# Hash attention with a feed-forward block: the first batch's value sums on GpSimd, with the order of the work made anew

## The chip, the cores and the metric

The kernel runs on one core of a Trainium2 chip. The core has five engines that run side by side, each through its own queue of instructions: TensorE (PE in the profile, with its weight loads as PEld), VectorE (DVE), ScalarE (ACT), GpSimd (POOL) and SyncE (SP), which here only issues DMAs. The metric is the device time of one execution in microseconds (us); lower is better.

## The reference

Four batches, eight heads, 768 positions, head size 64. Six random projections hash every query and key to a bucket; a query attends only to keys of its own bucket. Layer norm and a feed-forward block with a residual follow.

```python
q_bits = (np.einsum('bhsd,dk->bhsk', q, proj) > 0)      # k_bits alike
mask = q_bucket[:, :, :, None] == k_bucket[:, :, None, :]
scores = np.where(mask, scale * np.matmul(q, k.transpose(0, 1, 3, 2)), -1e9)
attn = np.exp(scores - scores.max(-1, keepdims=True))
attn = attn / (attn.sum(-1, keepdims=True) + 1e-09)
x = np.matmul(attn, v)                        # heads side by side: (4, 768, 512)
xn = (x - mu) / np.sqrt(var + 1e-06) * g_ln
out = x + np.maximum(xn @ w_ch1, 0.0) @ w_ch2   # 512 -> 2048 -> 512
```

Where no key shares a query's bucket, every score is -1e9 and the result is the plain mean of the values. The kernel reproduces this by adding 2^-100 times the sum of all values (and of as many ones) to every row of the attention product: it vanishes beside a real attention sum and decides where that is nothing. These sums of values over the keys, one vector for each head, are what the change is about.

## The kernel before

The work is cut into 12 query blocks u of 256 queries (three for each batch) and into two groups g of four heads. A step s of 72 takes one block, one group and one third of the keys. The whole kernel is one string, `ORDER` (lines 16 to 136), of words such as `A.t.5.2`: the operation, the engine whose queue it enters (t TensorE, v VectorE, a ScalarE, p GpSimd, s SyncE), and its arguments. The program walks through the words and emits each operation; so the string fixes the order in every engine's queue, and each engine takes its own words strictly in that order. Dependencies between engines are semaphores. `SLOTS` (139 to 163) says which of the few buffers of a kind (`pp` and `f` are PSUM places, `X`, `T`, `tp`, `vnat` and so on SBUF buffers) each new tile takes, in the order in which tiles are made.

The words that matter here, with the lines of their code:

- First batch, queries and keys: `lx` loads (370, buffers X), `tn` turns 32x32 blocks on DVE (375), `ca` casts to bfloat16 (382, the queue is the word's engine; the cast itself is line 311, 313 or 315), `ha` or `hc` multiply with the projections in float32 (392, 402), `bh`, `bc`, `sl`, `bi` make the sign bits from that (396 to 430).
- Later batches: `gx` (504) is a tiny GpSimd write that waits until an X buffer is free, `LX` (507) the load into it, `tu` the turning (510), `CA` the cast (518), `hm` the projection (521), `bt`, `mw`, `mr` the bits and their way through DRAM (534 to 551).
- Scores `S` (558), exponentials `E` in two halves (575), attention products `A` (587), and on DVE `na` (606, adds the value sums, empties the accumulator), `nb` (612, reciprocal and multiplication at line 617), `nc` and `ag` (statistics), `rs` (634, GpSimd: the inverse deviation), `ce` (626, centring), `fl` (638, a transposing DMA) or, for block 0, `ft` and `fc` through TensorE.
- Feed-forward: `F` (652) first product, `R` (662) ReLU on ACT or DVE, and for block 0 `D` and `Z` (669, 674), for the others seven smaller products `P`, `Y` (715 to 728) with sums of weights `sw` (688) and of activations `ss` (699). `lw1` and `lw2` load the quarters of the two weights through GpSimd's DMA queue (445, 456), `wg` scales a quarter of the first weight by the layer norm's gain (448). `O` writes results.
- Values: `lv` loads them (463), `cv` casts two heads to bfloat16 into `vaug` (469).

Value sums are made in two ways. `sq` (491), used for batch 0 only, multiplies a matrix of ones with each of the six pieces of the cast values on TensorE. `su` (477), used for batches 1 to 3, first adds the six pieces in float32 on GpSimd, and `sp` (486) then needs one ones product, which sums over the partitions. `sc` (496) copies either result from PSUM.

```python
    def su(eng, b, hs):
        ...
        nc.gpsimd.tensor_tensor(t3, s[:, 0:3], s[:, 3:6], op=AOP.add)
        nc.gpsimd.tensor_tensor(t3[:, 0], t3[:, 0], t3[:, 1], op=AOP.add)
        nc.gpsimd.tensor_tensor(
            vsum(b)[:, D * hs : D * (hs + 4)].rearrange("p (h d) -> p h d", d=D), t3[:, 0], t3[:, 2], op=AOP.add,
        )
    def sp(eng, b, hs):
        nc.tensor.matmul(
            ps(f"vp{b}{hs}", [P, 512], "f")[:, :256], ones, vsum(b)[:, D * hs : D * (hs + 4)], start=True, stop=True,
        )
    def sq(eng, b, hs):
        ...
        for kj in range(KJ):
            nc.tensor.matmul(p, ones, vaug(b)[:, hs : hs + 4, kj, 0:D], start=(kj == 0), stop=(kj == KJ - 1))
```

`wm` words are products of ones with ones that fill TensorE's queue during the first 11 us.

## Time and profile before

| | us |
|---|---|
| median of three runs | 294.56 (293.67 to 295.48) |
| the profiled execution | 294.45 |
| its span, first to last instruction | 292.7 |
| TensorE idle in the span | 8.2 |
| first feed-forward product group ready to go on (L657) | 36.79 |
| last product ends (L723) | 288.4 |

The granted TensorE clock was 0.999 over the span. A profile line names a source line, an engine, an operation, and output and input tiles with shapes; `x6` is a count, and an arrow in square brackets names what ended the engine's idle time before. "The chain of waits" is the profile's reconstruction, from the last instruction backwards, of what each step waited for. The tables of stretches give busy microseconds of each engine in a window; a busy TensorE need not be TensorE at its peak, since the ends of its pipelined products are modelled.

### The profile page before, as it was taken

The page shows a single profiled execution, that of the slowest core. Times are in us where ns is not written, and L with a number is a line of the kernel's source. Part 1 is how long each engine was busy: PE and PEld are TensorE (multiplying, and loading weights), DVE is VectorE, ACT ScalarE, POOL GpSimd, SP SyncE. Part 2 cuts the span into 40 slices and gives each one's busy share as a digit, 9 for nine tenths or more (in the row PEclk, how much of TensorE's full clock was granted, in tenths as well). Part 3 has the DMA queues.
Part 4 walks back from the last instruction along what each step waited for, and adds up shares of the span by engine and source line. Part 5 has one row for each costly group of instructions (what it writes and reads, how often), then busy time and mean ns, then how long its engine had stood idle before and what let it go on. Part 6 is the DMA issues. An engine that isn't in the chain of part 4 may idle for free.

```text
span 292.7 us, 10520 instructions
## 1 busy us (share of the span) xinstructions
PE 284.5 (97%) x4650; PEld 227.0 (78%) x4650; DVE 211.8 (72%) x475; ACT 199.8 (68%) x229; POOL 59.5 (20%) x94
## 2 busy tenths in 40 slices
PE   8999999999899999999999999999999999999994
PEld 4677778568688787888888878888888888898883
DVE  4889999876978978777577787467486566872543
ACT  2699898887956886775964996597784483715230
POOL 6353502133521100410510100602301000101000
PEclk9999999999999999999999999999999999999999
DMA  6996999589964580381930570130320201304032
GB/s 216 295 394 114 198 280 185 121 122 235 261 172 114 149 198 15 87 189 37 210 87 17 128 107 20 39 74 2 75 40 0 56 20 41 88 0 110 4 87 73
DMA packets 31055, 34.10 MB, mean 116 GB/s; under 512 B 15521, under 2 KB 27809, under 8 KB 31010
## 3 DMA queue, kind: packets, MB, share of 16 engines
q1 hardware_dynamic: 25938, 28.72, 39.1%
q0 software_dynamic: 4224, 4.19, 9.0%
q8 instruction: 36, 0.59, 0.8%
q10 hardware_dynamic: 848, 0.53, 0.7%
q14 instruction: 9, 0.07, 0.1%
HBM read 27.86 MB, written 6.88 MB: 119 GB/s over the span
## 4 chain that ended last, share of the span: by engine, by line
PE 92%; DVE 4%; DMA 2%; issue 0%
PE f L657 28%; PE sc L570 18%; PE X L723 13%; PE acc L595 12%; PE Yb L723 7%; PE Ya L723 3%; PE f L672 3%; PE hp L526 2%; DMA xnT<-xc 2%; PE hf L394 2%; PE warm L363 1%; DVE w_sb L454 1%; PE warm L366 1%; DVE x L617 1%; PE vp L494 0%; DVE st L621 0%
## 5 line engine op out<-in xcount | busy, mean ns | idle before, releaser
L576 ACT ACTIVATE E<-sc,bias_sb 128x1024 bf16<-128x1024 f32 x144 | 153.3, 1111 | 38.2 <-PE sc L570 35.5
L657 PE MATMUL f<-xnT,w_sb 128*128 128x256 bf16 x768 | 93.9, 273 | 1.9 <-DMA xnT<-xc 1.2
L657 PEld LDWEIGHTS <-w_sb 128*128 128x128 bf16 x768 | 71.8, 98 | 15.2 <-issue 4.5
L665 ACT ACTIVATE hb<-f 128x512 bf16<-128x512 f32 x64 | 37.9, 597 | 36.6 <-PE f L657 36.3
L570 PE MATMUL sc<-qb,kb 32*128 32x256 bf16 x1152 | 52.2, 267 | 0.0
L595 PE MATMUL acc<-vaug,E 128*128 128x65 bf16 x1152 | 43.4, 194 | 0.0
L595 PEld LDWEIGHTS <-E 128*128 128x128 bf16 x1152 | 40.7, 98 | 3.4 <-issue 2.5
L570 PE MATMUL sc<-G 6*128 6x256 bf16 (+1 forms) x576 | 41.5, 273 | 0.6 <-DVE G L307 0.5
L723 PEld LDWEIGHTS <-hb 128*128 128x128 bf16 x352 | 32.9, 98 | 6.0 <-issue 1.9
L635 POOL TENSOR_SCALAR rs<-mv 128x2 f32<-128x2 f32 x12 | 2.8, 232 | 157.7 <-DVE mv L624 157.7
L667 DVE TENSOR_SCALAR hb<-f 128x512 bf16<-128x512 f32 x32 | 21.8, 681 | 16.3 <-PE f L657 16.0
L728 DVE TENSOR_TENSOR x<-X,x 128x256 f32<-128x256 f32 x44 | 18.4, 421 | 18.1 <-PE X L723 17.9
L570 PEld LDWEIGHTS <-kb 32*128 32x128 bf16 x1152 | 30.2, 93 | 1.6
L723 PEld LDWEIGHTS <-S 128*128 128x128 bf16 x264 | 25.0, 98 | 4.7 <-issue 0.8
L570 PEld LDWEIGHTS <-G 6*128 6x128 bf16 (+1 forms) x576 | 15.2, 91 | 16.2 <-issue 13.5
L304 DVE STREAM_TRANSPOSE T<-X 128x384 f32<-128x384 f32 (+2 forms) x52 | 26.3, 539 | 0.0
L723 PE MATMUL Yb<-w_sb,S 128*128 128x256 bf16 x176 | 22.9, 273 | 0.0
L608 DVE SCALAR_TENSOR_TENSOR y<-vsB,acc 128x520 f32<-128x520 f32 x24 | 16.6, 690 | 7.4 <-PE acc L595 7.1
L723 PE MATMUL X<-wt,hb 128*128 128x256 bf16 x168 | 21.8, 273 | 0.0
L617 DVE TENSOR_TENSOR x<-y,rc 128x512 f32<-128x512 f32 x24 | 17.5, 731 | 0.8
L621 DVE BATCH_NORM_STATS2 st<-x 128x6 f32<-128x256 f32 x48 | 17.7, 412 | 0.2
L480 POOL TENSOR_TENSOR t<-vn 128x768 f32<-128x768 f32 x6 | 10.9, 1818 | 20.0 <-DMA vn<-in_v_dram 20.0
(92 smaller groups left out, 269.2 us busy)
## 6 DMA issues: line engine op xcount, KB each, us to landing
out_dram<-x SPq DMA_DIRECT2D x45, 128.0 KB
X<-in_k_dram SPq DMA_DIRECT2D x7, 768.0 KB
X<-in_q_dram SPq DMA_DIRECT2D x6, 768.0 KB
vn<-in_v_dram SPq DMA_DIRECT2D x24, 192.0 KB
w_sb<-in_moe_w_ch_dram POOLq DMA_DIRECT2D x8, 512.0 KB, 8.9
vn<-in_v_dram SPq DMA_DIRECT2D x2, 768.0 KB
X<-in_q_dram SPq DMA_DIRECT2D x2, 512.0 KB
Bd<-B SPq DMA_DIRECT2D x6, 96.0 KB
```

The costliest lines, as they stand in the source:

```text
L304: nc.vector.transpose(d[:, j], s[:, j, kj0 : kj0 + n])
L570: nc.tensor.matmul(sc(s, i // 2)[:, i % 2, 256 * kk : 256 * kk + 256], lh, rh, start=(rep == 0), stop=(rep == 2), skip_group_check=True,)
L576: nc.scalar.activation(E(s)[:, heads(h)], sc(s, h), AF.Exp, scale=EXP_SCALE, bias=bias_sb)
L595: nc.tensor.matmul(acc[:, qt, (D + 1) * i : (D + 1) * (i + 1)], E(s)[:, i, 256 * kk + P * qt : 256 * kk + P * qt + P], vaug(u // 3)[:, 4 * ...
L608: nc.vector.scalar_tensor_tensor(yt(u, g), vs, EPS_ROW, made[f"acc{u}{g}"][:, :, :A], op0=AOP.mult, op1=AOP.add,)
L617: nc.vector.tensor_tensor(xo, a[:, :, :, 0:D], rc.to_broadcast([P, 2, 4, D]), op=AOP.mult)
L621: nc.vector.bn_stats(stats(u)[:, qt, g], xt(u)[:, qt, 256 * g : 256 * g + 256])
L657: nc.tensor.matmul(f1[:, n].rearrange("p (t x) -> p t x", t=2), w1_sb[:, dt, P * nt : P * nt + P], xnT(u)[:, :, dt], start=(dt == 0), stop ...
L665: nc.scalar.activation(hb(u)[:, 2 * p : 2 * p + 2], f1, AF.Relu)
L667: eng.tensor_scalar_max(hb(u)[:, 2 * p : 2 * p + 2], f1, 0.0)
L723: nc.tensor.matmul(f2, lh[:, n], rh[:, n], start=(first and n == 0), stop=(n == 7), skip_group_check=True)
L728: nc.vector.tensor_tensor(x, made[f"{prod(u, k)}{u}"], x, op=AOP.add)
```

## The change

In batch 0 the two `sq` words are replaced by two `su` words on GpSimd and two `sp` words on TensorE. `ORDER` and `SLOTS` are written anew throughout: almost every line of the order differs, words move within their queues, and some change the engine (up to about 40 us: casts `ca.0.1.2`, `ca.1.1.2` from GpSimd and `ca.0.0.2` and the copy `bi.1.0.2` from ACT to DVE; `ca.1.1.0` from DVE to GpSimd; `ca.1.1.1`, `cv.0.0.2` and the ReLU `R.0.7` from DVE to ACT; `cv.0.4.0` from GpSimd to ACT). No function changes. The diff's first part and the buffers named here, cut:

```diff
@@ -16,147 +16,147 @@
...
-tn.v.1.1.1 ha.t.1.1.1 tn.v.1.0.0 E.a.1.1 gx.p.1.0.0 S.t.2.2 LX.s.1.0.0 E.a.2.0 ca.v.1.1.0 ha.t.1.0.0
-bh.v.1.1.1 ca.v.1.0.0 ha.t.1.1.0 ca.v.1.1.1 bh.v.1.0.0 cv.p.0.0.0 tn.v.1.1.2 cv.v.0.0.2 S.t.4.2 E.a.2.1
-E.a.4.0 E.a.4.1 gx.p.1.0.1 tn.v.0.0.2 ca.a.0.0.2 bh.v.1.1.0 A.t.2.2 sq.t.0.0 LX.s.1.0.1 sc.v.0.0
-A.t.1.2 A.t.0.2 ca.p.1.1.2 tn.v.0.0.1 ca.a.0.0.1 gx.p.1.1.1 S.t.3.2 ha.t.1.1.2 E.a.3.0 cv.p.0.4.0
-na.v.0.0 hc.t.0.0.1 nb.v.0.0 E.a.3.1 bh.v.1.1.2 bc.v.0.0.1 S.t.5.2 E.a.5.1 sl.t.0.0.1 tn.v.1.0.2
-bi.v.0.0.1 cv.p.0.4.2 sq.t.0.4 tn.v.1.0.1 E.a.5.0 sc.v.0.4 hc.t.1.0.2 S.t.8.2 E.a.8.0 gx.p.1.1.0
-tu.v.1.0.0.2 bc.v.1.0.2 hc.t.1.0.1 lw1.p.1 tu.v.1.0.0.3 A.t.4.2 tu.v.1.0.0.0 A.t.3.2 E.a.8.1 bc.v.1.0.1
-lw1.p.2 sl.t.1.0.1 bi.a.1.0.1 A.t.5.2 tu.v.1.0.0.1 tu.v.1.0.1.2 lw1.p.0 sl.t.1.0.2 bi.a.1.0.2 ca.a.1.0.1
...
-ce.v.0.0 ce.v.0.1 pmem.p rs.p.0 gt.t E.a.7.1 A.t.7.2 A.t.6.2 A.t.8.2 bt.v.1.0
-gc.v E.a.9.0 E.a.9.1 ft.t.0.1 fc.a.0.1 wg.v.1 ft.t.0.0 fc.a.0.0 lw2.p.1 S.t.10.2
-E.a.10.0 E.a.10.1 na.v.1.0 F.t.0.3 wg.v.3 wg.v.2 R.a.0.3 S.t.11.2 F.t.0.7 E.a.11.0
...
-lw2.p.0 S.t.12.2 R.a.0.6 na.v.1.1 lv.s.1.0.3 nb.v.1.1 E.a.12.1 CA.p.1.0.1 tu.v.1.1.0.2 mr.s.1.0.3
-E.a.13.0 lw2.p.3 mr.s.1.0.0 A.t.14.2 A.t.12.2 R.v.0.0 F.t.0.5 F.t.0.2 rs.p.1 tu.v.1.1.0.0
-tu.v.1.1.1.0 tu.v.1.1.0.1 ce.v.1.1 A.t.13.2 na.v.2.0 ca.a.1.0.2 nb.v.2.0 lw2.p.2 S.t.16.2 R.a.0.2
...
-nc.v.2.0 lv.s.1.0.1 sw.v.1.1 mr.s.1.1.2 A.t.17.2 A.t.15.2 E.a.18.1 A.t.16.2 na.v.2.1 D.t.0.1.2
-sw.v.3.0 mr.s.1.1.1 S.t.20.2 E.a.20.0 cv.a.1.0.2 nb.v.2.1 nc.v.2.1 E.a.20.1 D.t.0.0.2 D.t.0.0.3
-Z.v.0.0 S.t.19.2 E.a.19.0 D.t.0.1.3 Z.v.0.1 mr.s.1.1.0 E.a.19.1 fl.s.1.0 mr.s.1.1.3 lv.s.1.4.3
-su.p.1.0 F.t.1.4 R.v.1.4 lv.s.1.4.2 S.t.21.2 E.a.21.0 E.a.21.1 F.t.1.2 cv.p.1.0.0 LX.s.2.0.1
-R.a.1.2 lv.s.1.4.0 F.t.1.0 ag.v.2.1 R.a.1.0 A.t.20.2 sw.v.2.0 A.t.19.2 ag.v.2.0 rs.p.2
-ce.v.2.1 sw.v.4.1 ce.v.2.0 S.t.22.2 E.a.22.1 lv.s.2.0.1 LX.s.2.0.0 fl.s.2.1 sp.t.1.0 F.t.1.3
-R.a.1.3 sc.v.1.0 A.t.18.2 cv.a.1.4.2 na.v.3.0 tu.v.2.0.1.2 F.t.1.5 O.s.0.1 R.v.1.5 F.t.1.6
-R.v.1.6 sw.v.1.0 fl.s.2.0 E.a.22.0 nb.v.3.0 S.t.23.2 E.a.23.1 su.p.1.4 F.t.1.7 cv.v.1.4.0
-R.a.1.7 LX.s.3.1.0 E.a.23.0 tu.v.2.0.0.1 F.t.1.1 S.t.24.2 F.t.2.1 R.v.1.1 ss.v.1.1 ss.v.1.2
...
+sel.p tn.v.0.0.0 p32.p tn.v.0.1.0 on.p.1 lw1.p.3 ca.a.0.0.0 pmem.p ca.p.0.1.0 ha.t.0.0.0
...
+tn.v.1.1.1 E.a.1.0 ha.t.0.1.2 ha.t.1.1.1 bh.v.0.1.2 tn.v.1.1.0 ca.p.1.1.0 S.t.2.2 ca.a.1.1.1 tn.v.1.0.0
+ha.t.1.0.0 E.a.2.0 cv.a.0.0.2 bh.v.1.1.1 ca.v.1.0.0 bh.v.1.0.0 tn.v.1.1.2 ha.t.1.1.0 bh.v.1.1.0 tn.v.0.0.2
+tn.v.0.0.1 S.t.4.2 ha.t.1.1.2 cv.p.0.0.0 E.a.2.1 A.t.2.2 E.a.4.0 su.p.0.0 hc.t.0.0.1 bc.v.0.0.1
+A.t.1.2 bh.v.1.1.2 sl.t.0.0.1 E.a.4.1 ca.v.1.1.2 ca.a.0.0.1 cv.a.0.4.0 S.t.3.2 gx.p.1.0.1 sp.t.0.0
+bi.v.0.0.1 LX.s.1.0.1 A.t.0.2 E.a.3.0 su.p.0.4 gt.t sc.v.0.0 E.a.3.1 na.v.0.0 tn.v.1.0.2
+gc.v S.t.5.2 E.a.5.0 S.t.8.2 E.a.5.1 E.a.8.0 E.a.8.1 tn.v.1.0.1 nb.v.0.0 hc.t.1.0.1
+tu.v.1.0.0.1 sp.t.0.4 tu.v.1.0.0.3 tu.v.1.0.0.2 cv.p.0.4.2 A.t.4.2 bc.v.1.0.1 sl.t.1.0.1 bi.a.1.0.1 sc.v.0.4
+tu.v.1.0.0.0 tu.v.1.0.1.1 ca.a.1.0.1 tu.v.1.0.1.3 A.t.5.2 A.t.3.2 na.v.0.1 nb.v.0.1 lw1.p.2 tu.v.1.0.1.2
+S.t.6.2 E.a.6.0 hc.t.1.0.2 S.t.7.2 E.a.6.1 E.a.7.1 E.a.7.0 lw1.p.1 tu.v.1.0.1.0 hm.t.1.0
+S.t.9.2 E.a.9.0 nc.v.0.1 nc.v.0.0 bc.v.1.0.2 ag.v.0.0 sl.t.1.0.2 ag.v.0.1 A.t.7.2 ce.v.0.1
+bt.v.1.0 ce.v.0.0 bi.v.1.0.2 lw1.p.0 lw2.p.0 E.a.9.1 wg.v.2 A.t.6.2 A.t.8.2 na.v.1.0
+ft.t.0.1 fc.a.0.1 mw.s.1.0 mr.s.1.0.1 ft.t.0.0 fc.a.0.0 S.t.10.2 E.a.10.0 mr.s.1.0.0 wg.v.3
+hc.t.0.0.2 bc.v.0.0.2 F.t.0.4 S.t.11.2 R.v.0.4 ca.v.0.0.2 E.a.10.1 sl.t.0.0.2 bi.v.0.0.2 wg.v.0
...
+S.t.16.2 mr.s.1.0.3 E.a.16.1 lv.s.1.0.3 ag.v.1.1 ag.v.1.0 E.a.16.0 rs.p.1 R.a.0.6 A.t.14.2
+lw2.p.1 A.t.12.2 lv.s.1.0.1 F.t.0.5 lv.s.1.4.2 tu.v.1.1.0.0 R.a.0.5 tu.v.1.1.1.3 tu.v.1.1.1.0 lw2.p.2
+A.t.13.2 tu.v.1.1.0.2 tu.v.1.1.0.3 S.t.15.2 tu.v.1.1.0.1 E.a.15.1 lw2.p.3 tu.v.1.1.1.2 na.v.2.0 E.a.15.0
...
+na.v.2.1 nb.v.2.1 sw.v.3.1 sw.v.1.0 S.t.20.2 E.a.20.0 D.t.0.1.2 D.t.0.0.2 mr.s.1.1.1 cv.v.1.0.0
+D.t.0.0.3 E.a.20.1 S.t.19.2 E.a.19.1 E.a.19.0 Z.v.0.0 LX.s.2.0.1 cv.p.1.0.2 su.p.1.0 D.t.0.1.3
+nc.v.2.1 Z.v.0.1 LX.s.2.1.0 lv.s.1.4.3 lv.s.1.4.1 F.t.1.4 R.a.1.4 S.t.21.2 E.a.21.1 nc.v.2.0
+ag.v.2.1 ag.v.2.0 sw.v.2.0 F.t.1.2 R.v.1.2 F.t.1.0 E.a.21.0 R.v.1.0 A.t.18.2 lv.s.1.4.0
+A.t.20.2 rs.p.2 ce.v.2.0 ce.v.2.1 fl.s.2.1 sw.v.1.1 F.t.1.3 R.a.1.3 fl.s.2.0 sw.v.2.1
+sw.v.4.1 O.s.0.3 A.t.19.2 sp.t.1.0 sc.a.1.0 S.t.22.2 F.t.1.6 E.a.22.0 E.a.22.1 na.v.3.0
+F.t.1.5 S.t.23.2 E.a.23.0 R.v.1.6 R.v.1.5 F.t.1.7 F.t.1.1 R.a.1.7 E.a.23.1 R.v.1.1
+S.t.24.2 E.a.24.1 E.a.24.0 tu.v.2.0.1.2 LX.s.2.0.0 LX.s.2.1.1 F.t.2.1 O.s.0.0 cv.p.1.4.0 cv.v.1.4.2
...
-    T="011001100110",
-    X="0123021302312012",
-    rs="012102102102",
-    vnat="01010101",
-    vsum="000",
...
+    T="011001011010",
+    X="0123021302310312",
+    rs="012012012012",
+    vnat="01010110",
+    vsum="0000",
...
```

GpSimd's queue up to the second batch, before and after:

```
before: on.0 sel p32 on.1 lw1.3 ca.0.1.0 ca.0.1.1 ca.0.1.2 gx.1.0.0 cv.0.0.0 gx.1.0.1 ca.1.1.2 gx.1.1.1 cv.0.4.0 cv.0.4.2 gx.1.1.0
        lw1.1 lw1.2 lw1.0 pmem rs.0 lw2.1 lw2.0 CA.1.0.1 lw2.3 rs.1 lw2.2 CA.1.1.1 su.1.0 cv.1.0.0 rs.2
after:  on.0 sel p32 on.1 lw1.3 pmem ca.0.1.0 ca.0.1.1 gx.1.0.0 ca.1.1.0 cv.0.0.0 su.0.0 gx.1.0.1 su.0.4 cv.0.4.2
        lw1.2 lw1.1 lw1.0 lw2.0 CA.1.0.1 gx.1.1.1 gx.1.1.0 rs.1 lw2.1 lw2.2 lw2.3 rs.0 cv.1.0.2 su.1.0 rs.2
```

TensorE's queue around the replaced products, before and after:

```
before: S.4 A.2 sq.0.0 A.1 A.0 S.3 ha.1.1.2 hc.0.0.1 S.5 sl.0.0.1 sq.0.4 hc.1.0.2 S.8 hc.1.0.1 A.4 A.3 sl.1.0.1 A.5 sl.1.0.2 S.6 hc.0.0.2 sl.0.0.2
        S.7 hm.1.0 S.9 gt A.7 A.6 A.8 ft ft S.10 F.0.3 S.11
after:  S.4 ha.1.1.2 A.2 hc.0.0.1 A.1 sl.0.0.1 S.3 sp.0.0 A.0 gt S.5 S.8 hc.1.0.1 sp.0.4 A.4 sl.1.0.1 A.5 A.3 S.6 hc.1.0.2
        S.7 hm.1.0 S.9 sl.1.0.2 A.7 A.6 A.8 ft ft S.10 hc.0.0.2 F.0.4 S.11
```

More of the change, by code (lines that the diff above doesn't have):

```diff
@@ new lines @@
+S.t.57.2 ss.v.6.3 sc.a.3.0 E.a.57.1 fl.s.7.0 F.t.7.5 R.a.7.5 Y.v.6.1 na.v.9.0 P.t.6.6
+Y.v.6.6 S.t.59.2 E.a.57.0 E.a.59.1 E.a.59.0 P.t.6.5 Y.v.6.5 P.t.6.7 Y.v.6.7 S.t.60.2
+E.a.60.0 P.t.6.3 nc.v.8.1 P.t.6.4 ag.v.8.1 A.t.59.2 Y.v.6.3 ag.v.8.0 sp.t.3.4 Y.v.6.4
+O.s.6.2 rs.p.8 E.a.60.1 sc.v.3.4 S.t.61.2 E.a.61.1 E.a.61.0 F.t.7.6 R.v.7.6 A.t.58.2
+A.t.57.2 nb.v.9.0 F.t.7.4 S.t.64.2 F.t.7.0 R.a.7.4 E.a.64.0 na.v.9.1 nb.v.9.1 R.v.7.0
+A.t.60.2 nc.v.9.1 E.a.64.1 F.t.7.7 R.a.7.7 F.t.7.2 R.v.7.2 S.t.62.2 E.a.62.1 nc.v.9.0
@@ new lines @@
+F.t.7.1 ce.v.8.0 fl.s.8.0 R.a.7.1 F.t.7.3 R.a.7.3 ss.v.7.1 A.t.61.2 P.t.7.2 P.t.7.1
+E.a.62.0 ss.v.7.2 S.t.63.2 Y.v.7.2 ce.v.8.1 ag.v.9.1 E.a.63.1 O.s.6.1 fl.s.8.1 E.a.63.0
+Y.v.7.1 A.t.62.2 na.v.10.0 P.t.7.5 Y.v.7.5 P.t.7.6 ss.v.7.4 ss.v.7.3 S.t.65.2 E.a.65.1
+P.t.7.3 Y.v.7.6 Y.v.7.3 P.t.7.7 O.s.6.3 Y.v.7.7 S.t.68.2 E.a.68.1 E.a.68.0 ag.v.9.0
+rs.p.9 P.t.7.4 Y.v.7.4 F.t.8.7 F.t.8.1 R.a.8.1 A.t.63.2 A.t.64.2 R.v.8.7 F.t.8.0
+R.v.8.0 E.a.65.0 F.t.8.2 A.t.65.2 ce.v.9.0 R.a.8.2 F.t.8.6 R.a.8.6 O.s.6.0 F.t.8.3
```

182 lines of the change are left out of this document (84 added, 98 removed).

## The prediction

> **What bounds the kernel now.** I read the page's busy shares first, then the table of ten-microsecond stretches, then TensorE's waits, and last the timelines of single engines around the places where TensorE waited.
>
> ```profile
> PE 284.5 (97%) x4650; PEld 227.0 (78%) x4650; DVE 211.8 (72%) x475; ACT 199.8 (68%) x229; POOL 59.5 (20%) x94
> ...
> PE 92%; DVE 4%; DMA 2%; issue 0%
> ```
>
> TensorE is busy or on the chain of waits nearly all the time, so the time is its queue plus its idle time: 292.7 - 284.5 = 8.2 us. Of these 1.11 us lie at the start and 4.3 us after the last product (ends 288.4, span ends 292.7). TensorE's waits hold the rest:
>
> ```profile
> PE f L657 <- DMA xnT<-xc: 1.2, 1, 1.2
> PE sc L570 <- DVE G L307: 0.5, 1, 0.5
> PE f L657 <- DVE w_sb L454: 0.4, 1, 0.4
> PE hf L418 <- DVE Bc L307: 0.3, 1, 0.3
> PE f L657 <- ACT xnT L648: 0.2, 1, 0.2
> ```
>
> All but the first fall between 20 and 37 us, and there the stretches (columns: TensorE, weight loads, DVE, ACT, POOL, clock, DMA share, GB/s) show a second engine at its limit:
>
> ```profile
> 20.00:30.00 10.00, 9.08 (x242) 6.81 (x246) 9.39 (x24) 9.35 (x13) 4.68 (x8) 1.00 0.75 179
> 30.00:40.00 10.00, 9.39 (x190) 7.26 (x183) 9.96 (x26) 9.19 (x11) 5.04 (x6) 1.00 1.05 220
> ```
>
> So up to 37 us the kernel is a race of TensorE, DVE (9.96 of 10) and ACT (9.19); from there to the end it is TensorE alone, with one wait at 78.6 us. The products that the change replaces run in the race (TensorE's timeline: start, length, count):
>
> ```profile
> 17.34 0.83 PE L494 MATMUL vp<-vaug,ones 128*128 128x256 bf16 x6
> ...
> 22.79 0.83 PE L494 MATMUL vp<-vaug,ones 128*128 128x256 bf16 x6
> ```
>
> **TensorE's share.** In the chain each six products take 0.67 to 0.68 us, 0.112 us each. Twelve go (-1.35), two come (+0.22): -1.13 us. Both groups stand ahead of waits for DVE (0.54 us at 21.90, 0.35 at 28.50, 0.17 and 0.44 before 36.79). A product removed ahead of such a wait only lengthens it, so the 1.13 us count only as far as DVE and ACT come earlier too.
>
> **POOL's share.** Each sum is three additions, in the rows of the later batches 1818, 838 and 781 ns (the fastest 1805, 728, 725): 3.3 to 3.4 us. Two of them are +6.9 us; against that one cast of `vaug` (0.83, to ACT) and one of `kb` net (1.08) leave. POOL was busy 3.40 + 4.68 of the 20 us from 10 to 30, so 5.0 us more fit. The first cast of values waited 3.74 us for its DMA and started at 14.99, so: cast to 15.8, first sum to 19.2. The second half landed at 20.14 (that cast waited too): sum to 23.5, cast `cv.p.0.4.2` to 24.4. Behind the first sum waits `gx.p.1.0.1` and with it SP's load of batch 1's keys, 16.98 before, about 19.3 now. The hardware queue moved 0.35 to 0.43 MB in every microsecond up to 22 us, so that load stood behind others anyway; its first reader starts at about 26 us. If that cover failed, it would cost up to 2.3 us. Behind the second sum wait the three w1 loads, 24.20 before, 24.4 now: hidden, since their data moved from 26 to 34 us and the quarter needed first is now issued first. `pmem` moved to the front falls into 1.39 us of POOL's idle time before 5.97.
>
> **ACT's share up to 37 us.** It gains a `kb` cast (0.63), two casts of 128x768 and a ReLU of F.0 (0.60), and loses a `qb` cast (0.63) and a copy of bits (0.39). The trace has no 128x768 cast on ACT; between its 128x512 (0.63) and 128x1536 (1.49) casts a straight line gives 0.85, and those two are the bounds. Sum +1.9 us (1.5 to 3.2). From 9.95 to 37.00 ACT was busy 24.92 of 27.05 us: it just fits, so ACT allows little more than is forecast. One place hurts: `cv.a.0.4.0` stands ahead of E.3 and cannot start before 20.14. E.3 then runs 21.0 to 23.1 (before 20.02 to 22.14), E.5.0 ends at 24.1, and S.8, which needs its PSUM place, ends at 25.0 (before 24.8).
>
> **DVE's share up to 37 us.** In: casts 0.62 + 0.42 + 0.62, a copy 0.42. Out: casts 0.62 + 0.62 + 0.52, a ReLU 0.69. Net -0.4. Larger is what it stops waiting for. Four w1 scalings whose median is 344 ns took 3.55 us, while POOL issued DMAs and cast:
>
> ```profile
> 33.44 3.55 DVE L454 TENSOR_SCALAR w_sb<-w_sb,gT 128x512 bf16<-128x512 bf16 x4
> ...
> 33.42 1.60 POOL L457 DMA_DIRECT2D w_sb<-in_moe_w_ch_dram  x2
> 35.00 1.58 POOL L315 CAST kb<-T 128x1536 bf16<-128x1536 f32 x1
> ```
>
> Two of the four took 1.55 us each, 2.4 us lost, and the first feed-forward product group stood behind them until 36.79. The new order issues `lw2.p.0` straight behind the w1 loads, lets the cast CA.1.0.1 follow at about 30 us, and puts the other w2 loads behind `rs.p.1`. POOL should then be idle when the scalings run, and they cost 1.4 us.
>
> **Laying it together.** After S.8 (25.0): hc 0.4, the sums' product 0.1 (its sum ready at 23.5), A.4, A.5, A.3 and sl 1.6, to 27.2 (before 26.9). DVE takes na.0.1 (0.66) at 27.3 to 27.8, nb.0.1 (0.89), two turnings (1.0): 30.3. The second half of hm.1.0 (0.73) needs these: S.9 at 31.05 (31.40 before). DVE goes on with statistics, centring and bits (3.1 us), to 33.4, and w1's quarter (1.4), to 34.8. TensorE after 31.05: S.9 0.77, sl 0.13, three A 1.47, ft 0.55, S.10 0.77, hc 0.38: 35.1. So the first F starts at about 35.2, against 36.57 (36.79 less the two products already done, 0.22): -1.4. What follows on TensorE is the same work plus one sl (0.13): -1.25 us. For each earlier time I take the row nearest to it; two or three such steps can each miss by 0.7, so this term lies between -2.6 (scalings, the 0.65 us that one multiplication lost at 20.17, little else in the way) and +0.3.
>
> **The wait at 78.6 us.** It was the transposing DMA of x of query block 2, issued at 71.73, 6.3 us after Z.0.1 started (65.39). In the new order both DMAs follow each other behind R.1.0: from Z.0.1 on, three F and S steps to F.1.0's end 3.5, ReLU 0.7, two centrings 1.1, one DMA issue 1.25: 6.6 us. TensorE's work from Z.0.1 to the waiting F.2.1 stays 12 us. So the wait is not cured: +0.3 us, between -1.24 (gone) and +1. Other edits (R, casts and copies moved between DVE and ACT, another order of F, P and outputs) lie after 37 us beside a full TensorE; ACT is at 68% and DVE at 72%, so they count nothing. Were that cover gone at one of them, it would cost that instruction, 0.4 to 1.5 us. The tail has the same last steps, four outputs come nearer to it; 0 to +0.5 us, I take 0.
>
> **Sum.** 294.45 (the profiled run: span 292.7 and 1.75 around it) - 1.25 + 0.3 = 293.5 us. The median of the three runs is 294.56, 0.11 above the profiled one.
>
> **Rivals.**
>
> *All of it is gained.* The first F comes 2.6 us earlier and the 1.24 us wait goes: 294.45 - 3.8 = 290.6. For: the waits exist. Against: ACT's 2.1 us of room, and the DMA issue worked out above. Chance 0.17.
>
> *The saving becomes waiting.* DVE or ACT sets the first F where it was; the product count changes nothing: 294.2 to 295.3. For: DVE at 9.96 of 10. Against: the 2.4 us of stalled scalings. Chance 0.17.
>
> *POOL's additions hold up DVE.* At 20.17 a multiplication of two SBUF operands (L617) took 1.34 us in place of 0.69 while POOL cast from 20.14 to 20.96. During the sum at 73.4 a subtraction took 1.14 in place of 0.67, an L617 0.98 and a cast 1.08 in place of 0.52. In the new order the cast ca.1.1.2 and nb.0.0's L617 may meet additions; by these rows 0.3 to 0.65 each, as much as the one collision that goes, so I count 0. The Trainium skill (SBUF — State Buffer, "SBUF: two separate sides") speaks against the change: the port pair that GpSimd and VectorE share is locked for a whole instruction and the other engine fully blocks. By that rule both could lose a whole first addition. If both do, DVE's chain loses 2 x 1.82 - 0.65 = 3.0 us and the time is 296.5; with one, 294.7. Chance 0.10, as the additions should be over or nearly so (19.2, 23.5) when the two come (19.5, 23.4).
>
> *Slower: w2 arrives late.* `lw2.p.1`, `.2` and `.3` were issued at 33.4, 48.7 and 36.5; now all three stand behind `rs.p.1`, which waits for statistics, 47.7 before, about 46 to 47 now. A single load at 48.69 had its data by 54 to 55. Three at the best rate seen (0.19 MB per us, 0.52 MB each) land by 57 us. At the rate of 36 to 50 us (1.57 MB in 14 us) the last lands at 62, and the subtraction sw.3.1, due at 58.8 on DVE, holds Z, the statistics and the transposing DMA of block 2, which is already the late one: +3.7 us, 297.2, and up to 298.5 with TensorE's own wait at D.0.0.3 (due 61.4). It decides once the last quarter lands after 58.8. Chance 0.24.
>
> The forecast keeps 0.32.
>
> **How the numbers follow.** About 1% is what a measurement can tell from no change: below 291.6 or above 297.5. Faster: the first rival less a little, 0.15. Slower: most of the w2 rival, 0.20. Within: 0.65. The likeliest case has 292.6 to 294.3; the range reaches to 290.8 and 297.7, leaving out the best of the first and the worst of the last rival.
>
> **What would show it.** Right: two vp products, scalings of 0.34 us each with POOL idle beside them, the first F at 34.5 to 36 us, a wait for xnT of 1 to 2 us near 77. Wrong: a TensorE wait on L487 (POOL's sums late), L617 or the kb cast over 1.3 us before 26 us, DVE waiting for w_sb before 60 us, or new waits of TensorE after 80 us, where I count none.

## The result, and the profile after

The changed kernel takes 297.27 us (median of 20 executions, 294.66 to 298.94), the kernel before 295.00 (20 executions beside it, 293.67 to 297.38). The ratio on record is 1.0048 with a 95% interval of 1.0026 to 1.0069: slower by half a per cent, where the forecast was faster by 0.4%. It is not the ratio of the two medians (1.008): the changed kernel's times lie in two groups, 8 of them from 294.66 to 296.27 us and 12 from 296.89 to 298.94, and the last section shows what part TensorE's clock has in that. Ratios and medians of the runs below leave out single executions more than 1.5% above the fastest of the same kernel. The profiled execution after took 297.77 us, with a span of 295.7 (before 294.45 and 292.7).

The page's busy shares and the first line of its chain of waits, after:

```profile
PE 284.5 (96%) x4640; PEld 226.8 (77%) x4640; DVE 210.0 (71%) x479; ACT 201.9 (68%) x231; POOL 59.2 (20%) x94
...
PE 89%; DVE 4%; DMA 3%; issue 2%; SPq 1%; ACT 1%; DVEq 0%
```

Ten products fewer (4640 for 4650), the same 284.5 busy us in a span 3.0 us longer: the products are gone, and between its first and its last product TensorE stands idle for 5.8 us in place of 2.8. "issue", time in which the engine waited for nothing that the profile shows, has gone from 0% to 2% of the chain. TensorE's waits after (engine, line, what it waited for: sum, times, longest):

```profile
PE sc L570 <- issue: 2.1, 2, 1.6
PE sc L570 <- ACT E L576: 1.6, 2, 0.9
PE warm L363 <- DVE bias_sb L320: 1.1, 1, 1.1
PE f L657 <- DMA xnT<-xc: 0.9, 1, 0.9
PE acc L595 <- issue: 0.5, 1, 0.5
PE hf L418 <- DVE Bc L307: 0.4, 1, 0.4
```

Of the waits of before, that for Bc (0.3, now 0.4 us) and the start's are left; the largest of the new ones has no releaser. The two stretches that were a race of three engines, after:

```profile
20.00:30.00 10.00, 7.99 (x218) 6.35 (x210) 9.55 (x24) 9.30 (x11) 6.93 (x8) 1.00 0.80 198
30.00:40.00 10.00, 7.85 (x200) 5.65 (x190) 7.72 (x24) 7.71 (x9) 1.54 (x3) 1.00 0.88 148
```

TensorE was busy 9.08 and 9.39 us there before. From 30 to 40 us VectorE and ScalarE are now *less* busy (7.7 each), and neither of TensorE's two long stops in that stretch (0.56 and 1.58 us) is put down to them. VectorE's scalings of the first weight are as cheap as forecast (four in 1.13 us, 3.55 before), and still the first F starts at 36.62 us:

```profile
33.97 1.13 DVE L454 TENSOR_SCALAR w_sb<-w_sb,gT 128x512 bf16<-128x512 bf16 x4
...
36.62 1.05 PE L657 MATMUL f<-xnT,w_sb 128*128 128x256 bf16 x8
...
37.94 0.27 PE L570 MATMUL sc<-G 32*128 32x256 bf16 x3
39.79 0.28 PE L570 MATMUL sc<-G 32*128 32x256 bf16 x1 [1.58 <-issue]
```

The last two lines are step S.11: three of four products of one kind run, then 1.58 us of nothing, then the fourth. A wait for a buffer splits such four products two and two, as that of S.8 for E does (two at 22.77 us, two at 23.92); three and one fits none, and something else stops the queue here. From 85 us on, each score step ahead of which the same work has run lies a constant 2.88 us later than before; the loss is complete by then.

**Counting the queue.** Counted in order of start, products and weight loads alike (and the 24 semaphore and drain instructions that the trace keeps), the stops without a releaser lie at places 961 (S.9, 0.56 us), 1217 (S.11, 1.58) and 1729 (A.13, 0.50) of TensorE's queue: 193 + 256 k. The DMA part of the page has a row for instructions, the same before and after:

```profile
q8 instruction: 36, 0.59, 0.8%
```

36 packets of 16 KB, for some 9300 instructions: 256 in each. So TensorE's instructions arrive in blocks, by DMA; a border is the place where one block ends and the next begins. From the trace's packets (a block's request is taken to be the crossing of the border before):

| kernel, place | border before crossed | packet starts | lands | crossed | TensorE waits |
|---|---|---|---|---|---|
| after, 961 | 26.92 | 30.75 | 31.69 | 32.99 | 0.56 |
| after, 1217 | 32.99 | 37.41 | 38.39 | 39.79 | 1.58 |
| after, 1729 | 45.50 | 50.60 | 51.91 | 53.44 | 0.50 |
| before, 961 | 25.75 | 28.55 | 29.50 | 30.95 | under 0.15 |
| before, 1217 | 30.95 | 34.07 | 35.02 | 37.71 | 0 |
| before, 1729 | 43.75 | 47.79 | 49.09 | 50.54 | under 0.15 |

Of the borders up to 93 us in all runs, none was crossed less than 1.25 us after its packet had landed; 1.3 to 1.5 us marks one that came too late or only just in time. What the DMA engines did while the block for 1217 was due (33.0 to 37.3 us, then 37.3 to 38.5; packets, MB, share of 16 engines, above 100% since packets overlap):

```profile
q0 software_dynamic: 742, 0.73, 106.7%
q1 hardware_dynamic: 116, 0.08, 6.0%
...
q0 software_dynamic: 13, 0.01, 6.2%
q8 instruction: 1, 0.02, 5.1%
q1 hardware_dynamic: 20, 0.01, 4.5%
```

q0 is GpSimd's queue with the weights. The instruction packet moves when these are through. The new order has put a second-weight load straight behind the three first-weight loads (24.05 to 27.1 us), so the queue stays full to 37 us. The weights are not the only load that does this: while the block for 1729 was due (45.5 to 50.6 us), q0 moved nothing, and SyncE's loads filled the 16 engines.

**SyncE.** Its queue after, around 60 us:

```profile
56.96 0.34 SPq L544 DMA_DIRECT2D Bd<-B  x1
62.39 2.10 SPq L547 DMA_DIRECT2D G<-Bd  x3
64.53 0.44 SPq L467 DMA_DIRECT2D vn<-in_v_dram  x1
65.07 2.62 SPq L639 DMA_TRANSPOSE xnT<-xc  x2
```

The value load lv.1.0.0 and the transposing DMAs fl.1.1 and fl.1.0 stand behind three mr.1.1 reads, which wait for the bits' way through DRAM (5.4 us here). Before, that value load and fl.1.1 were issued ahead of the reads, at 56.25 to 57.26 us. F.1.4 now waits 0.85 us for xnT, and VectorE stands 3.24 us in front of the cast of these values, with Z behind it.

### The profile page after: what moved, and what is told of

It is laid out like the page before. It is cut to its first block, busy times and chain, and to the rows that moved or that the text cites. A ratio compares the mean times of both kernels' runs of the same rounds, so it can differ in the third digit from the quotient of the medians.

```text
span 295.7 us, 10524 instructions
## 1 busy us (share of the span) xinstructions
PE 284.5 (96%) x4640; PEld 226.8 (77%) x4640; DVE 210.0 (71%) x479; ACT 201.9 (68%) x231; POOL 59.2 (20%) x94
## 4 chain that ended last, share of the span: by engine, by line
PE 89%; DVE 4%; DMA 3%; issue 2%; SPq 1%; ACT 1%; DVEq 0%
PE f L657 29%; PE sc L570 17%; PE X L723 13%; PE acc L595 11%; PE Yb L723 7%; PE Ya L723 3%; PE hp L526 3%; PE hf L394 3%; DMA Bd<-B 2%; PE warm L363 1%; DMA xnT<-xc 1%; ACT E L576 1%; SPq L547 1%; DVE S L708 1%; DVE T L304 1%
## 5 line engine op out<-in xcount | busy, mean ns | idle before, releaser
L665 ACT ACTIVATE hb<-f 128x512 bf16<-128x512 f32 x67 | 39.5, 597 | 31.3 <-PE f L657 31.1
L570 PE MATMUL sc<-G 6*128 6x256 bf16 (+1 forms) x576 | 42.1, 273 | 3.4 <-issue 1.6
L595 PE MATMUL acc<-vaug,E 128*128 128x65 bf16 x1152 | 44.4, 194 | 0.5 <-issue 0.5
L667 DVE TENSOR_SCALAR hb<-f 128x512 bf16<-128x512 f32 x29 | 19.9, 687 | 13.5 <-PE f L657 13.1
L617 DVE TENSOR_TENSOR x<-y,rc 128x512 f32<-128x512 f32 x24 | 17.2, 717 | 0.8
L480 POOL TENSOR_TENSOR t<-vn 128x768 f32<-128x768 f32 x8 | 14.8, 1852 | 0.2
```

The source lines that it names most:

```text
L570: nc.tensor.matmul(sc(s, i // 2)[:, i % 2, 256 * kk : 256 * kk + 256], lh, rh, start=(rep == 0), stop=(rep == 2), skip_group_check=True,)
L595: nc.tensor.matmul(acc[:, qt, (D + 1) * i : (D + 1) * (i + 1)], E(s)[:, i, 256 * kk + P * qt : 256 * kk + P * qt + P], vaug(u // 3)[:, 4 * ...
L617: nc.vector.tensor_tensor(xo, a[:, :, :, 0:D], rc.to_broadcast([P, 2, 4, D]), op=AOP.mult)
L665: nc.scalar.activation(hb(u)[:, 2 * p : 2 * p + 2], f1, AF.Relu)
L667: eng.tensor_scalar_max(hb(u)[:, 2 * p : 2 * p + 2], f1, 0.0)
```

## The experiments

Theory F: the loss is TensorE's late instruction blocks (F does not stand for the words `F` here). Theory Q: it is SyncE's order. The rivals: A, ScalarE sets the pace (the two waits for E at 23.9 and 29.5 us); P, GpSimd's additions hold up VectorE. Ratios are against the kernel before in the same batch of runs (medians 294.85 to 295.33), with 95% intervals. Most rows rest on 10 or 12 executions, those of e6 and e18 on 6, that of e9 on 4.

| run | what is different | median, us | ratio |
|---|---|---|---|
| e1 | changed kernel again | 296.43 | 1.0041 (1.0014 to 1.0068) |
| e2 | new order, old sums | 296.38 | 1.0036 (1.0012 to 1.0060) |
| e3 | old order, new sums | 297.16 | 1.0069 (1.0039 to 1.0099) |
| e11 | e3, a cast on ScalarE | 297.46 | 1.0091 (1.0062 to 1.0120) |
| e5 | two casts on GpSimd | 295.65 | 1.0007 (0.9988 to 1.0026) |
| e4 | second weight behind rs.p.1 | 296.69 | 1.0040 (1.0008 to 1.0073) |
| e7 | second weight held to 37 us | 295.70 | 1.0024 (1.0005 to 1.0044) |
| e6 | SyncE's order, first try | 298.42 | 1.0101 (1.0070 to 1.0133) |
| e8 | e6 and e7 | 296.18 | 1.0051 (1.0024 to 1.0078) |
| e10 | SyncE's order, second try | 295.66 | 1.0011 (0.9986 to 1.0035) |
| e14 | e10 and e7 | 294.53 | 0.9981 (0.9959 to 1.0002) |
| e12 | e10, e7 and e5 | 295.67 | 1.0009 (0.9982 to 1.0036) |
| e18, e9 | changed, borders moved by 64, 128 | 300.67, 298.84 | 1.0168 (1.0128 to 1.0208), 1.0101 (1.0059 to 1.0142) |
| e19 | e14, borders moved by 128 | 296.28 | 1.0030 (1.0002 to 1.0058) |
| e17, e15 | before, borders moved by 64, 128 | 295.49, 293.74 | 1.0014 (0.9980 to 1.0048), 0.9947 (0.9923 to 0.9970) |
| e16 | before, SyncE and TensorE, two moves | 294.59 | 0.9981 (0.9961 to 1.0002) |

### The two halves of the change

e1 is the changed kernel as it is.

> The changed kernel once more, unchanged. In its trace TensorE idles 0.56, 1.58 and 0.50 us with no releaser ('issue'), each time in front of a queue position 193 + 256k (961, 1217, 1729 counted over weight loads and products), 1.30 to 1.53 us after a 16 KB packet of the instruction queue has landed. Theory F (instruction fetch: TensorE's queue is refilled in blocks of 256 instructions, and the block comes late while weights are loaded): gaps again only at such positions, again 1.3 to 1.5 us after a packet, 2 to 3.5 us in sum in an execution near 297.5 us and under 1 us in one near 295. Theory A (ScalarE's gate: the exponential E.3 behind a cast that waits for values): the waits for E at S.8 and S.7, 0.86 and 0.69 us, are there in every execution, and gaps without releaser lie anywhere. Ratio to the kernel before 1.003 to 1.008 by either.

Its profiled execution took 297.27 us and has stops of 0.29 and 1.05 us at 961 and 1217 and none at 1729. The places are those of theory F, but the sum, 1.3 us, is under the 2 to 3.5 that it expected at such a time; the two waits for E stand (0.86 and 0.69 us), and that for xnT is 1.19 us long.

e2 puts the six ones products back in the new order:

```diff
-su.p.0.0  -sp.t.0.0  +sq.t.0.0
-su.p.0.4  -sp.t.0.4  +sq.t.0.4   (cv.p.0.4.2 ahead of it)
```

> The new order with the six ones products put back for both halves of the first batch and no additions on GpSimd (the cast of the last two heads goes ahead of the second six). Theory F and theory A put the loss into the order: the loss stays and the 1.13 us of products come on top as far as they do not fall into waits, 296 to 298.5 us. Theory P (GpSimd's additions hold up VectorE): L617 at 23.4 us falls from 1.29 to 0.7 us and the time to 294 to 295.5 us.

e3 puts the sums into the old order (su.p.0.0 behind the cast cv.p.0.0.0, su.p.0.4 ahead of cv.p.0.4.0, sp.t.0.0 and sc.v.0.0 behind S.3):

```diff
 cv.p.0.0.0 +su.p.0.0 ... -sq.t.0.0 ... S.t.3.2 +sp.t.0.0 ... +su.p.0.4 cv.p.0.4.0 +sc.v.0.0
-sq.t.0.4 +sp.t.0.4
```

> The old order with the additions on GpSimd and one product each; the first product goes behind S.3, the second sum goes ahead of the casts of the second half's values. Nothing else moves. Theories F and A: 293.7 to 295.5 us, the product saving (1.13 us) partly eaten by a TensorE wait of about 0.8 us at the second sum and by the casts that come 3.3 us later on GpSimd. Theory P: 296 us or more, with L617 or casts on VectorE over 1.3 us.

The order alone is as slow as both together (1.0036 and 1.0041): in the new order the sums on GpSimd neither help nor hurt by what can be measured. TensorE's waits in e2, three of its lines:

```profile
PE f L657 <- DMA xnT<-xc: 2.2, 3, 1.0
PE sc L570 <- ACT E L576: 1.8, 2, 1.1
PE acc L595 <- issue: 0.3, 1, 0.3
```

Here nothing stops at 961 or 1217, and one stop of 0.28 us stands at 1985; what is long are the waits for E and for xnT. With the products of the kernel before and this one stop, e2 is still 1.1 us slower than that kernel, so the late blocks can't be the whole loss. That e2 and e1 take the same time may be chance: e1's stops are 1.1 us longer, as much as the ten products are worth.

In the old order the sums cost about 2 us, as theory P expected (296 us or more, with a cast over 1.3 us). There, VectorE and GpSimd show, in e3 (VectorE's cast, GpSimd's addition, VectorE's copy of the sums):

```profile
16.47 1.71 DVE L475 CAST vaug<-vn 128x768 bf16<-128x768 f32 x1
...
15.96 1.81 POOL L480 TENSOR_TENSOR t<-vn 128x768 f32<-128x768 f32 x1
...
20.76 0.43 DVE L502 COPY vsB<-vp 128x256 f32<-128x256 f32 x1 [0.91 <-PE vp L487]
```

The cast, 0.52 us before, begins inside the addition and ends 0.41 us after it (15.96 + 1.81 = 17.77; 16.47 + 1.71 = 18.18): it stood still for the whole rest of the addition. That agrees with the rule of the Trainium skill (SBUF — State Buffer, "SBUF: two separate sides") that the prediction weighed; what the prediction lacked is that the place of the second start inside the first engine's instruction decides the price: here 1.19 us, between the 0.3 to 0.65 that it took from its rows and the whole addition of 1.82. The third line is a second price: the sum is ready later than six products were, and the copy stands ahead of the sign bits in VectorE's queue.

e11 takes the collision away:

```diff
-cv.v.0.0.2
+cv.a.0.0.2
```

> The kernel of before with the sums on GpSimd, as in the run with the sums alone, but the value cast cv.0.0.2 is on ScalarE (behind E.2.0) in place of VectorE. Theory P (GpSimd's first addition and VectorE's cast of values lock each other out: that cast took 1.71 us in place of 0.52): the cast takes about 0.8 us on ScalarE, TensorE's wait of 1.03 us at 18.2 shrinks to under 0.4 and that of 1.44 us at 23.4 to about 0.5; 1 to 1.5 us less than with the sums alone, ratio 1.002 to 1.004 in place of 1.007. Rival (the cast was late for another reason, such as its data or its queue): the waits stay, ratio 1.006 to 1.008.

```profile
20.37 0.42 DVE L502 COPY vsB<-vp 128x256 f32<-128x256 f32 x1 [2.11 <-PE vp L487]
```

The cast takes 0.84 us on ScalarE and TensorE's wait of 1.03 us for it shrinks to 0.23, as P expected; but VectorE then waits 2.11 us for the sums where it waited 0.91, S.5 still waits (1.68 us), and nothing is gained. P, in the form "the lock costs the time", falls. That the lateness of the sum is the price that counts in the old order is read from these waits and not tested by itself; in the new order the bits stand ahead of the copy, which waits only 0.23 us.

### ScalarE or the blocks: e5

```diff
-cv.a.0.0.2  -cv.a.0.4.0
+cv.p.0.0.2 (behind cv.p.0.0.0)  +cv.p.0.4.0 (ahead of cv.p.0.4.2)
```

> The changed kernel with two casts of values (cv.0.0.2 and cv.0.4.0) moved from ScalarE to GpSimd, the rest as it was. Theory A (ScalarE sets the pace at 24 and 29.5 us: TensorE waited 0.86 and 0.69 us for exponentials): both waits shrink to under 0.3 us, the first F starts 1 us earlier or more, and the time falls by about 1 us, to a ratio near 1.001 against the kernel before. Theory F (TensorE's instructions arrive late, in blocks of 256): the two waits may go, but the waits at queue positions 961 and 1217 grow by as much, since the blocks come no earlier; ratio unchanged at 1.003 to 1.005. Cost to be watched: GpSimd's second sum or the value cast comes 0.5 to 1 us later and the w1 loads are issued at about 25.5 in place of 24.1 us.

```profile
PE sc L570 <- ACT E L576: 1.8, 2, 1.1
PE warm L363 <- DVE bias_sb L320: 1.1, 1, 1.1
PE f L657 <- DMA xnT<-xc: 0.6, 1, 0.6
```

About 1 us was won, but not for A's reason: the two waits for E are still there (1.10 and 0.69 us), although ScalarE has now idle time ahead of E.3 (0.82 us) and E.5 (0.30). What went are the waits without a releaser. The casts put the weights 2 us later on GpSimd's queue (26.02 in place of 24.05), the border at 27.19 is crossed ahead of most of them, and that block starts 0.12 us later (3.83 after). The gain goes with the stops, by an accident of GpSimd's queue. A falls in the form tested, that ScalarE's casts make the two waits; the waits themselves are in every version of the new order.

### Moving the weight: e4 and e7

e4 moves the load that fills 33 to 37 us behind `rs.p.1`; e7 holds it only until about 37 us, by a copy that reads a tile made then:

```diff
 e4: -lw2.p.0 (behind lw1.p.0)  +lw2.p.0 (behind rs.p.1)
 e7: -lw2.p.0                   +hold.p +lw2.p.0 (behind gx.p.1.1.0)
+    def hold(eng):
+        nc.gpsimd.tensor_copy(junk2, Bc(0, 0, 2)[:, 0:1])
```

> The changed kernel with the load of the second weight's first quarter moved behind rs.p.1, to the other three; it takes one of four quarter loads (about 2.6 us of DMA time) out of the stretch from 26 to 37 us. Theory F: the instruction packet that started 4.4 us after its block border (37.41 against 32.99) starts within 3 us, and the gap of 1.58 us at position 1217 is gone or under 0.4 us; 0.5 to 1.5 us faster than the changed kernel. Theories A and P: that gap stays or moves at random, and the time is that of the changed kernel within 0.5 us, or up to 1 us slower since the first quarter now comes late for D.0.1.0.

> The changed kernel with the first load of the second weight (lw2.p.0) held on GpSimd, by a copy of one column of the tile Bc of block 2, until about 37 us; it was issued at about 27. Theory F: the instruction block that is asked for at 33 us no longer queues behind that load, its packet starts under 2 us after the border in place of 4.4, and the wait at position 1217 (1.05 to 1.58 us) goes; the weight is still there for the first D at 55 us, so the 2.4 us wait of the run with the load behind rs.p.1 does not appear; about 1.0 us less, ratio near 1.001. Rival (the waits without a releaser are lost records or a clock matter, not the supply of instructions): the wait at 1217 stays at over 0.8 us.

In e4 the packet for 1217 starts 1.12 us after the border in place of 4.42 and S.11 no longer waits; but the first D waits for the weight itself, 2.8 us in two pieces (the longer 2.37). In e7 the packet starts 1.12 us after the border too, now without that price. From 33 to 37.3 us e7 shows the instruction packet inside the window in which it is missing above:

```profile
q0 software_dynamic: 294, 0.28, 40.1%
q1 hardware_dynamic: 144, 0.10, 7.2%
q8 instruction: 1, 0.02, 1.7%
```

The wait at 961 stays (0.77 us), as it must: nothing ahead of it was moved. 0.5 to 0.7 us were won for 1.0 expected, which is not clear of noise: e7's interval (1.0005 to 1.0044) reaches into those of the changed kernel (from 1.0014 and 1.0026). That this load makes this block late is shown; what the block costs in time is not.

### SyncE's order: e6, e10

```diff
 e6:  LX.s.1.1.1 LX.s.1.1.0 ahead of mr.s.1.0.1 mr.s.1.0.0
      fl.s.1.1 fl.s.1.0 ahead of mr.s.1.1.0 mr.s.1.1.2 mr.s.1.1.3 lv.s.1.0.0
 e10: lv.s.1.0.0 behind lv.s.1.0.1
      fl.s.1.1 fl.s.1.0 ahead of mr.s.1.1.0 mr.s.1.1.2 mr.s.1.1.3
```

> The changed kernel with the words of one queue alone in another order: on SyncE the loads LX.1.1.1 and LX.1.1.0 go ahead of mr.1.0.1 and mr.1.0.0, and the transposing DMAs fl.1.1 and fl.1.0 ahead of mr.1.1.0, .2, .3 and lv.1.0.0. Theory Q (these DMAs stood behind waits for bits from DRAM): VectorE's wait of 1.73 us for the load at 51.0 goes, fl.1.1 is issued at 61 to 62 in place of 65 us, and TensorE's wait of 0.85 us for xnT at 69.1 goes; time about 0.9 us less, ratio near 1.0015. Theory F: the waits at 961 and 1217 stay (0.3 to 0.6 and 1.0 to 1.6 us), so at least 1.3 us of the loss stays. If what was saved at 69 us comes back at another wait for xnT near 77 us, theory Q is right on the place and wrong on the price.

> The changed kernel with SyncE's queue alone edited: the value load lv.1.0.0 is issued behind lv.1.0.1 (about 45 us in place of 64.5) and the transposing DMAs fl.1.1 and fl.1.0 ahead of mr.1.1.0, .2 and .3 (about 60 us in place of 65). Theory Q in its second form (both the transposing DMAs and this value load stand behind mr's waits; VectorE's cast of the values, which the load holds, holds Z, and Z the feed-forward block's PSUM place): VectorE's wait of 3.2 us at 64 us is gone, Z.0.0 starts at about 65.5 in place of 67.9, and F.1.4 waits for neither xnT nor Z (under 0.2 us); 0.8 us less than the changed kernel, ratio about 1.002, if no wait for xnT comes back near 77 us; with that wait (up to 1.2 us) no gain. Theory F alone: the waits at 961 and 1217 stay.

e6 was a miss: 1.6 to 1.8 us *slower* than the changed kernel, and all six of its executions hold a dip of TensorE's clock, worth about 1.7 us (last section). fl.1.1 goes at 56.92 us and the wait for xnT is gone, but the value load still stands behind the reads (64.68), VectorE waits 3.79 us for it, and Z, behind that cast, is late by so much that F.1.4 waits 2.10 us for Z to free its PSUM place. Two causes lay on one wait; with one gone, the other sets it. e10 moves both: Z.0.0 starts at 66.33 (67.88 after), F.1.4 waits less than 0.15 us, and no wait for xnT comes back:

```profile
PE sc L570 <- issue: 1.9, 2, 1.0
PE sc L570 <- ACT E L576: 1.5, 2, 0.9
PE warm L363 <- DVE bias_sb L320: 1.1, 1, 1.1
PE hf L418 <- DVE Bc L307: 0.4, 1, 0.4
```

About 1 us against the changed kernel, with intervals that overlap again (0.9986 to 1.0035). The waits go as Q's second form says, and the stops of F stay (0.82 and 1.03 us), as both theories said.

### Do they add up: e8, e14, e12

> The two edits before together, SyncE's order and the held weight load. If F and Q each hold and add up: about 1.9 us less than the changed kernel, ratio near 0.998. If the block that is late next takes the place of the one removed: the sum of the two is not reached, ratio 1.000 to 1.003, and waits at 961, 1473 or 1729 show where.

> The changed kernel with two of the three edits: the first load of the second weight held until about 37 us, and SyncE's queue with the value load and the transposing DMAs ahead of mr; the value casts stay on ScalarE. If the two causes (a late block of instructions at 1217, SyncE's order) are separate and add up: no wait at 1217 and none near 69 us, 1.7 us less than the changed kernel, ratio 0.998 to 1.000. If a next block takes the place (961 stays, 1473 or 1729 appears, as in the run with three edits): ratio 1.000 to 1.002.

> The changed kernel with three edits together: the two value casts on GpSimd, the first load of the second weight held until about 37 us, and SyncE's queue with the value load and the transposing DMAs ahead of mr. If the late instruction blocks and SyncE's queue are the whole loss: no wait at 961, 1217 and 1729, none at 69 us, and the time falls below that of the kernel before by the TensorE work removed, 0.5 to 1.1 us: ratio 0.996 to 0.999. If a wait that is next in line takes over (ScalarE's two of 0.7 to 1.1 us stay, xnT near 77, or the second weight late at D): ratio 1.000 to 1.003.

e8 carries e6's fault (1.8 us in front of F.1.4) and settles nothing more. e14 adds e7 to e10: 0.9981, 1.8 to 2.0 us less than the changed kernel's 1.0041 to 1.0048, about what the two bring alone (0.5 to 0.7, and 0.9 to 1.1), and at or just below the kernel before. This gain is clear of noise: e14's interval ends at 1.0002, those of the changed kernel begin at 1.0014 and 1.0026. So the held load and SyncE's order together take back the loss; how it divides between them is not settled. The stops at borders are not gone, they have moved on (0.26, 0.69, 0.77 and 0.25 us at 1217, 1473, 1729 and 1985; the profile puts the second down to VectorE), and their sum is 2.0 us, against 2.6 in the changed kernel's profile and 1.3 in e1's: the stops do not account for most of what e14 wins. e12 adds e5's casts and lies above e14, by less than the intervals can tell, with waits for GpSimd (0.43 and 0.36 us) and one of 0.49 us at 1217.

### Moving the borders: e9, e15, e17, e18, e19

Here the work stays as it is and only the count changes: the 8 warming products of 512 columns become 72 of 56 (or 40 of 102). They take as long (3.54 us for 3.60), and each later instruction moves 128 (64) places down the queue.

```diff
-        for _ in range(NWARM):
-            nc.tensor.matmul(wp[:, 0].rearrange("p (a x) -> p a x", x=P), ones, row(4, P), start=True, stop=True)
+        for _ in range(72):
+            nc.tensor.matmul(wp[:, 0, :56], ones, ones[:, :56], start=True, stop=True)
```

> The changed kernel with the 8 warming products of 512 columns at the start replaced by 72 of 56 columns: about the same 3.6 us, but every later TensorE instruction moves 128 places (64 products and 64 weight loads) down its queue, half a block. Nothing else differs. Theory F (TensorE's instructions arrive in blocks of 256, and a block asked for while weights are being loaded comes late): the waits without a releaser move to other words; none at S.9 and S.11 (old positions 961 and 1217), and where there are any, they lie at the new positions 193 + 256 k, that is at old 833, 1089 or 1601 (about 29.5, 36 and 48.5 us). The border at about 24 us falls before or into the issue of the w1 loads, so the first block should be less late than in the changed kernel. Rival (these waits belong to the words S.9 and S.11, by their data or buffers): waits of 0.3 to 0.6 and 1.0 to 1.6 us stay in front of S.9 and S.11. The time can go either way.

```profile
33.38 0.55 PE L644 MATMUL ft<-ident,xc 128*128 128x128 bf16 x7
34.78 0.22 PE L644 MATMUL ft<-ident,xc 128*128 128x128 bf16 x1 [0.84 <-issue]
```

In e9's profile S.9 and S.11 run without a stop; the only stop without a releaser in the queue there sits between the seventh and the eighth turning product of ft, which is place 1217 of the new count (1089 of the old). The stop belongs to the place in the queue, not to the step. That settles that F's stops exist and that the place in the queue makes them, not what they cost.

> The kernel of before with the same 72 short warming products in place of 8 long ones, so that its instruction blocks end half a block earlier in the work; a control for the run of the changed kernel with that edit, whose time rose to a ratio of 1.010. Theory F: the borders fall on other words, and the kernel of before loses what its own borders happened to spare it, or not: any waits without a releaser lie at positions 193 + 256 k. If the ratio is near 1.010 less 0.0045 as well, the loss of that run comes from the short products or from borders that meet the loads in both orders; if it is under 1.002, it belongs to the changed order.

> The kernel of before with 40 warming products of 102 columns in place of 8 of 512: the blocks end 64 instructions earlier in the work (half of the shift that gave a ratio of 0.995). Theory F (when a block is asked for, beside which loads, decides 1 to 2 us of the time): the time differs from both the kernel before and the one shifted by 128, by anything from 0.994 to 1.006, and waits without a releaser, if any, lie at positions 193 + 256 k. Rival (the gain of the run with 72 products came from the short products at the start, the clock or the first 10 us): the ratio is 0.994 to 0.997 here too, with no block later than before.

> The changed kernel with the same 40 warming products of 102 columns. Theory F: waits without a releaser leave S.9 and S.11 and lie at positions 193 + 256 k, that is at old 897, 1153, 1409 or 1665; the time lies anywhere from 0.999 to 1.010. Rival (the rise to 1.010 of the changed kernel shifted by 128 came from the short products): the ratio is about 1.010 here too.

> The changed kernel with the second weight's first load held, SyncE's order mended, and 72 short warming products (shift of 128 instructions). If borders and edits are independent and the shift costs this order what it cost the changed kernel (about 0.5%): ratio 1.002 to 1.004. If the shift's cost came from the loads that the edits move: ratio 0.994 to 0.998, and the waits at borders are under 0.5 us in all.

The same edit made the kernel before *faster* by 0.5% and the changed kernel slower by another 0.5%; the half shift left the kernel before where it was, by its interval, and made the changed one slower by 1.2%. The rival of e17 falls: short products by themselves win nothing. The two rises of the changed kernel are less sure than their intervals say, since 3 of e9's 4 executions and 5 of e18's 6 hold a dip of TensorE's clock (last section); the one execution of each without a dip took 297.00 and 298.08 us. The latter is 1.010, so e18's rival is not ruled out. F's stops don't account for the sizes: e15's profile has no stop at a border, and the kernel before had none over 0.15 us either; e17, no faster, has one of 0.65 us at place 1217, which its profile puts down to ScalarE. What went in e15 is the wait of 1.24 us for xnT at F.2.1 (TensorE gets there at 77.32, as before, and the DMA has landed) and most of that of 0.54 us at S.5. The trace shows the last of its packets (256 bytes each) at 76.5 us in place of 77.9: it is issued only 0.2 us earlier, but the loads of values and queries ahead of it in SyncE's queue go out 0.9 us earlier (66.46 for 67.36). What moved those no run tells. In e18's profile F.1.4 waits 2.72 us for xnT, the wait that SyncE's order sets; with that order mended (e19) the full shift costs about 0.5% (1.0030 for e14's 0.9981), and there only 1 of 12 executions holds a dip.

### A wait of before, taken alone: e16

```diff
 fl.s.2.0 ahead of O.s.0.1;  A.t.22.2 ahead of F.t.2.1
```

> The kernel of before with two moves: on SyncE the transposing DMA fl.2.0 goes ahead of the output O.0.1, behind which it was issued at 71.73 us, and on TensorE the attention product A.22 goes ahead of F.2.1, which waited 1.24 us for that DMA. If the wait is simply the DMA's issue time: fl.2.0 is issued at about 71.05, A.22 fills 0.49 us, and the wait falls to under 0.2 us; 1.0 to 1.2 us less than before, ratio 0.996 to 0.997, and nothing later is late. Rival (a later block, ReLU or product takes the wait): ratio 0.999 to 1.001.

F.2.1 no longer waits; in this profile two other waits stand at that place, 0.69 us for E and 0.88 for A's values (VectorE's cast). 0.6 us were won, between the two expectations, and the interval just reaches no change.

A version that beats both kernels is e15: 293.74 against 295.15 us (294.94 for the executions of the kernel before that hold no dip of the clock; e15's twelve hold none).

## Why the prediction was wrong, by its own steps

- **"Other edits … lie after 37 us beside a full TensorE … so they count nothing"**: this failed, and with the sign. With SyncE's order taken back and one weight load held (e14) the changed kernel is 1.8 to 2.0 us faster and no slower than before. A full TensorE hid neither: it was fed by SyncE's DMAs and by its own instruction blocks, and the working followed neither queue behind 37 us beyond w2 and block 2's transposing DMA. The step also looked past the three mr.1.1 reads now ahead of fl.1.1, though the word order showed them.
- **The first F at 35.2 us, -1.25**: at 36.62, so nothing was gained up to here. The sums, the casts and the scalings came as worked out, and S.8, with its wait of 0.86 us for E, ended at 24.75 (25.0 expected). Of the 1.4 us, 0.56 is the block at 961, and S.9 itself was 0.66 late (31.71 for 31.05): the working took VectorE's chain to S.9 alone, and TensorE's own way there was longer, by the 0.69 us that S.7 waited for E. "Saving becomes waiting" is what happened: up to the first F TensorE idles 2.5 us in place of 1.5, and the products that left were worth 1.1.
- **+0.3 for the wait at F.2.1**: it is gone there, and 0.85 us stand at F.1.4, a block earlier, for DMAs that the working did not follow.
- **New waits after 80 us: none** — right.
- **w2 late**: the second to fourth quarter were issued at 50.38 (rs.p.1 at 49.38, 46 to 47 expected), yet VectorE waited only 0.23 us and TensorE not at all. The rival fell on its price; the weight that hurt was the *first* quarter, issued early, by what it held up.
- **POOL's additions hold up VectorE**: counted at 0, and in the new order right: one L617 took 1.29 us in place of 0.69 (beside a cast), as much as the collision that went.

The profiled time is 4.3 us over the forecast: 1.4 for the first F, 2.1 for the blocks at 1217 and 1729, less 0.7 at xnT (0.85 for the 1.54 in the sum), makes 2.8. Of the other 1.5 us, 0.3 lie outside the span (2.07 us around it, 1.75 before). The rest goes with TensorE's busy time, which is the same in both profiles although 1.1 us of products are gone; up to the first F it had fallen, and between 37 and 91 us that came back in stretches too short for a line. Why stays unexplained.

## What to carry to other kernels

A saturated engine still depends on queues that its busy share does not show: when a change moves bulk loads, look at where the instruction packets land, and count the queue where it stops without a releaser. Of a queue in strict order, follow each wait that a word is moved behind to the end of its line of readers; when one edit removes a wait and nothing is won, look for a second cause on the same wait. And measure a reordering at two or three shifts of the instruction count before you believe half a per cent.
